# Regrouped out-projection rows, a new order of the last projection chunks and GpSimd remainders in a four-layer attention and Fourier kernel

## The chip, the cores and the metric

The kernel runs on one core of a Trainium2 chip. The metric is device time in microseconds (us) of one execution; lower is better. [...] TensorE (PE in the profile) multiplies, VectorE (DVE), ScalarE (ACT) and GpSimd (POOL) do elementwise work, and SyncE (SP) issues all the DMAs of this kernel from one queue, in order. Each engine takes its own instructions in the order in which the program lists them.

## The reference

Four layers on one sequence of 2048 rows of 640 numbers, all in float32: attention, Fourier, attention, Fourier, each with a residual.

```python
def _A_ref(x, wqkv, wo):
    B, S, D = x.shape
    H = 32; Dh = D // H; W = 256
    ...
    scores = jnp.einsum("bhqd,bhkd->bhqk", q, k) * (Dh ** -0.5)
    ...
    mask = (idx[:, None] - idx[None, :] >= 0) & (idx[:, None] - idx[None, :] < W)
    scores = jnp.where(mask[None, None], scores, -1e9)
    p = _softmax(scores, axis=-1)
    o = jnp.einsum("bhqk,bhkd->bhqd", p, v)
    return (lambda x, *d: x.transpose(*d))(o, 0, 2, 1, 3).reshape(B, S, D) @ wo
...
x = x + _A_ref(_layernorm(x, axis=-1), A_wqkv, A_wo)
x = x + _B_ref(_layernorm(x, axis=-1), B_dft_seq_re, B_dft_seq_im, B_dft_hid_re, B_dft_hid_im)
```

`_B_ref` is a Fourier mix: a product with two 640x640 matrices, then with two 2048x2048 matrices, and the real part. The change lies in the attention layers alone.

## The kernel before, in words

**Products.** Each float32 operand is kept as a high part, rounded to the matmul's fp32r, and a remainder (`lo = x - hi`); a product is three matmuls, hi*hi, hi*lo and lo*hi. To make such a pair, one engine casts and another subtracts: `split` (L220) does both at once, `cut_job` (L212) queues the cast on ScalarE and then, by `sub_job` (L198), the subtract on VectorE ("dve") or on GpSimd ("pool", there in two halves of the columns).

**The attention layer.** `before_heads` (L364) normalizes, transposes, makes the values v and chunks 0 and 1 of the q and k projection. `heads` (L597) holds the rest. The 32 heads go in 8 quads of four. A quad has 16 query blocks of 128 rows, and the loop over `step` (L770) handles one block a step: at step t the scores of block t+10 with rows as output (`s_head`, L617, matmul L622, running row maximum on VectorE at L627), the transposed scores of block t (`t_pair`, matmul L650), their exponential on ScalarE (`t_exp`, L660), the band mask on GpSimd (`t_mask`, L666 and L670), and for block t-1 the product with v (`pv`, matmul L685, copied out at L692). 128 steps plus 10 ahead make the stage. Scores and values share six PSUM banks, and the order in which they are taken is written down by a small planner (`borrow`, L136) with assumed holding times. After four blocks `finish` (L696) stores the quad's unnormalized output (`od`) and the reciprocal of its sums (`rd`) and notes (quad, block of 512 columns) in `stored`.

**Fill.** Between these matmuls `fill` (L745) puts others that the heads do not wait for. `more` (L731) takes them from three generators in turn. `project` (L559) makes the remaining chunks 2 to 9 of q and k, each for four column blocks of 512 (sb 0 to 3), two blocks at a time (`pieces`, L523): 30 pairs of matmuls (L253), about four a step. `partials` (L946) multiplies the first three of five 128-row chunks of the attention output by their rows of the output weights, for 16 tiles of 128 sequence rows, and adds x (L970). `late` (L1024) adds the other two chunks, then normalizes for the Fourier layer. What remains of `late` after the last step runs in `after_heads` (L1103) among the first Fourier matmuls (L1360). `due` (L717) says at which step which part of the projection has to be done, since `pack` (L573) reloads q and k of a quad, two chunks wide, eight steps before their use.

**A finished piece** (`copied`, L537): ScalarE copies it out of PSUM (L540) to one of five raw tiles (`raw`, L158), GpSimd casts it (L543), VectorE subtracts (L207), SyncE stores it (L520) and `packable` is noted.

**Queued work.** `tick` (L172) runs once per half step. It runs what `post` (L166) has put off by so many half steps, and then takes at most one job from each of three lanes, ScalarE, VectorE and GpSimd. Since engines take instructions in order, a job's place in this order is its place in the engine's queue.

**Chunks of the attention output.** Its 640 rows are sorted into five chunks of 128 (`CHUNKS`, L45) as rectangles of heads by coordinates. `load_o` (L835) loads one chunk for one block (L855) with the reciprocals broadcast to the same rows (L861), scales it in two halves on GpSimd (L885) seven half steps later, and cuts it. It waits until all quads of the chunk are in `stored`: chunks 0 and 1 need quads 0 to 3, chunk 2 quads 4 and 5, chunk 3 quads 6 and 7, chunk 4 all eight. Two sets of buffers serve blocks 0 and 1, and then again blocks 2 and 3. `prepare` (L909) loads the weights for the partial products when chunk 9 begins, cuts them and asks for block 0 when chunk 9's second half begins, and loads the first four tiles of x when the projection ends (`load_y`, L941).

## Time and profile before

| | us |
|---|---|
| median of 3 runs | 2223.3 (2220.41 to 2227.0) |
| the profiled execution | 2220.75 |
| its span, first to last instruction | 2219.0 |
| mean granted TensorE clock | 0.991 |
| first attention layer, head steps 0 to 127 | 159.22 to 535.59 |
| second attention layer, head steps 0 to 127 | 1260.74 to 1636.29 |

A row of a windows view has the stretch in us from the span's start and its length, then the busy time of TensorE's matmuls, of its weight loads, of VectorE, ScalarE and GpSimd, each with its number of instructions in brackets, and last the granted clock of TensorE (1.00 is full), the mean busy share of the 16 DMA engines and their GB/s. A row of a group has line, engine and operation, out<-in with the shapes, the count, then busy us and mean ns of one, and the idle time before it with what ended it. In the view of a single line the three numbers are the shortest, median and longest duration in ns. In a waits view the three numbers are total us, times and the longest one. A timeline row has start, duration, engine, line.

### The profile page before, as it was taken

How to read it: one execution, taken by the hardware profiler on the slowest of the kernel's cores; microseconds unless marked ns; L12 is line 12 of the kernel's file. 1: busy time of each engine (PE TensorE's matmuls, PEld its weight loads, DVE VectorE, ACT ScalarE, POOL GpSimd, SP SyncE). 2: the span in 40 equal slices, each digit the busy share in tenths (PEclk: the TensorE clock that was granted, in tenths of full speed). 3: DMA queues.
4: the chain of work that ended last, by engine and by line, in shares of the span. 5: the costliest groups of instructions: out<-in, count | busy, mean ns of one | idle time of the engine just before them, and what ended most of it. 6: DMA issues, size and time to landing. Idle time of an engine off the chain costs nothing.

```text
span 2219.0 us, 49084 instructions
## 1 busy us (share of the span) xinstructions
PE 2131.4 (96%) x17908; PEld 1786.0 (80%) x17908; DVE 1669.5 (75%) x4031; ACT 1126.6 (51%) x2101; POOL 910.6 (41%) x1456
## 2 busy tenths in 40 slices
PE   7999999998989999999999999998989999999999
PEld 7987777677868888889999777776777688888899
DVE  7368888785897968776651788887858978687776
ACT  3127776656554545552431377676655545455332
POOL 3016565666613223232330266566665132341334
PEclk9999999899999999999999999999999999999999
DMA  5545565775435354665646456657855354546653
GB/s 196 176 160 190 182 190 192 225 208 175 142 124 176 128 185 133 215 202 193 205 147 191 151 189 183 199 184 225 211 160 157 115 182 137 174 143 216 223 169 120
DMA packets 220177, 392.11 MB, mean 177 GB/s; under 512 B 39200, under 2 KB 85792, under 8 KB 219936
## 3 DMA queue, kind: packets, MB, share of 16 engines
q1 hardware_dynamic: 219936, 388.98, 55.6%
q8 instruction: 141, 2.31, 0.5%
q14 instruction: 100, 0.82, 0.1%
HBM read 273.94 MB, written 113.77 MB: 175 GB/s over the span
## 4 chain that ended last, share of the span: by engine, by line
PE 70%; DVE 13%; issue 6%; DMA 4%; ACT 3%; POOL 3%; SPq 0%; ACTq 0%; DVEq 0%; POOLq 0%
PE banks L1360 28%; PE banks L235 13%; PE banks L253 9%; PE banks L685 5%; PE banks L650 5%; DVE banks L627 5%; PE banks L1648 4%; PE banks L622 4%; DMA qp<-qk_d 1%; DVE c L207 1%; POOL big L228 1%; DVE mc L627 1%; DMA qk_d<-c 1%; DVE qp L228 1%; PE banks L337 1%
## 5 line engine op out<-in xcount | busy, mean ns | idle before, releaser
L627 DVE CUSTOM_DVE_ANT_0 banks<-banks,mask 128x384 f32<-128x384 f32 (+2 forms) x1024 | 526.8, 556 | 98.5 <-PE banks L622 80.5
L660 ACT ACTIVATE pt<-banks 128x768 f32<-128x768 f32 (+2 forms) x512 | 394.3, 772 | 179.0 <-PE banks L650 74.0
L666 POOL TENSOR_SCALAR_AFFINE_SELECT pt<-pt 128x256 f32<-128x256 f32 x512 | 215.8, 422 | 282.0 <-ACT pt L660 243.2
L253 PE MATMUL banks<-big,wc 64*128 64x512 f32 x1920 | 271.2, 394 | 0.4 <-DVE pt L438 0.4
L650 PE MATMUL banks<-qp,kp 61*128 61x384 f32 (+2 forms) x1024 | 211.8, 383 | 32.5 <-DVE mc L627 28.5
L685 PE MATMUL banks<-pt,vq 128*32 128x128 f32 x5760 | 213.4, 280 | 1.5 <-ACT pt L660 1.5
L622 PE MATMUL banks<-kp,qp 60*128 60x384 f32 (+2 forms) x1024 | 204.9, 352 | 6.6 <-DVE mc L627 4.1
L670 POOL TENSOR_SCALAR_AFFINE_SELECT pt<-pt 128x256 f32<-128x256 f32 x448 | 207.2, 462 | 0.0
L253 PEld LDWEIGHTS banks<-big,wc 64*128 64x128 f32 x1920 | 186.5, 185 | 22.9 <-ACT x L540 1.7
L650 PEld LDWEIGHTS banks<-qp,kp 61*128 61x128 f32 x1024 | 108.6, 186 | 100.4 <-DVE mc L627 76.5
L685 PEld LDWEIGHTS banks<-pt,vq 128*32 128x32 f32 x5760 | 143.4, 110 | 49.5 <-issue 36.4
L222 ACT ACTIVATE c<-pt 128x512 fp32r<-128x512 f32 x150 | 93.6, 626 | 160.3 <-POOL pt L1280 52.9
L222 ACT ACTIVATE qp<-pt 128x512 fp32r<-128x512 f32 (+1 forms) x195 | 119.9, 624 | 105.3 <-DVE pt L1294 54.0
L228 DVE TENSOR_TENSOR c<-pt,c 128x512 fp32r<-128x512 f32 x150 | 123.0, 822 | 52.0 <-ACT c L222 49.9
L228 DVE TENSOR_TENSOR qp<-pt,qp 128x512 fp32r<-128x512 f32 (+1 forms) x191 | 151.2, 799 | 11.7 <-ACT qp L222 9.0
L1360 PE MATMUL banks<-qp,big 128*128 128x512 f32 x630 | 152.4, 394 | 2.9 <-POOL qp L228 1.7
L1293 POOL TENSOR_TENSOR pt<-pt,pt 128x512 f32<-128x512 f32 x34 | 50.7, 1490 | 237.1 <-DMA pt<-c 145.9
L622 PEld LDWEIGHTS banks<-kp,qp 60*128 60x128 f32 x1024 | 119.9, 188 | 32.1 <-DVE mc L627 19.5
L627 DVE DVE_READ_ACCUMULATOR2_ANT mc<- 128x1 f32 x1024 | 144.3, 141 | 0.0
L1360 PEld LDWEIGHTS banks<-qp,big 128*128 128x128 f32 x630 | 119.0, 190 | 28.8 <-POOL qp L228 2.3
L1360 PE MATMUL banks<-qp,xc 128*128 128x512 f32 x480 | 117.2, 390 | 0.7 <-DVE xc L228 0.7
L543 POOL CAST c<-x 128x512 fp32r<-128x512 f32 x64 | 40.3, 633 | 181.3 <-ACT x L540 180.3
(246 smaller groups left out, 4475.0 us busy)
## 6 DMA issues: line engine op xcount, KB each, us to landing
pt<-c SPq DMA_DIRECT2D x188, 512.0 KB
qk_d<-c SPq DMA_DIRECT2D x80, 512.0 KB
kp<-qk_d SPq DMA_DIRECT2D x384, 80.0 KB
qp<-qk_d SPq DMA_DIRECT2D x384, 80.0 KB
kp<-u_d SPq DMA_DIRECT2D x32, 640.0 KB
o_d<-ou SPq DMA_DIRECT2D x64, 256.0 KB
x_d<-x SPq DMA_DIRECT2D x48, 320.0 KB
v_d<-pt SPq DMA_DIRECT2D x16, 768.0 KB
```

The lines of the kernel that those rows point to most:

```text
L222: nc.scalar.activation(hi, src, AF.Copy, scale=-1.0 if neg else 1.0)
L228: (eng or nc.vector).tensor_tensor(out=lo, in0=src, in1=hi.bitcast(F32), op=OP.subtract)
L235: self.nc.tensor.matmul(p, x, y, start=n == 0, stop=n == last)
L253: self.nc.tensor.matmul(ps[a], x[r], y[r], start=half + i == 0, stop=half == 1 and i == n - 1, skip_group_check=True)
L622: nc.tensor.matmul(p, qp[quad % 2][b:b + 60, z, qb * P:(qb + 1) * P], kp[quad % 2][b:b + 60, z, k0 * P:(qb + 1) * P], start=True, stop=True)
L627: nc.vector.tensor_tensor_reduce(out=p, in0=p, in1=self.mask[:, 384 - n * P:], scale=1.0, scalar=NEG, op0=OP.add, op1=OP.max, accum_out=mc ...
L650: nc.tensor.matmul(self.banks[:, banks[e], :n * P], kp[quad % 2][b:b + 61, z, kb * P:(kb + 1) * P], qp[quad % 2][b:b + 61, z, kb * P:(kb + ...
L660: nc.scalar.activation(pt[quad, kb][:, 2 * z:2 * z + 2, :n * P], self.banks[:, b0:b1 + 1, :n * P], AF.Exp, scale=SCALE)
L666: nc.gpsimd.affine_select(out=t[:, :, 0:P], in_=t[:, :, 0:P], pattern=[[0, 2], [1, P]], compare_op=OP.is_ge, fill=0.0, base=0, channel_mul ...
L670: nc.gpsimd.affine_select(out=t[:, :, 256:384], in_=t[:, :, 256:384], pattern=[[0, 2], [-1, P]], compare_op=OP.is_gt, fill=0.0, base=0, ch ...
L685: nc.tensor.matmul(self.banks[32 * h:32 * h + 32, bank, :P], vq[:, 96 * (kb % 4) + 21 * h:96 * (kb % 4) + 21 * h + 32], t[:, h, (qb - kb) ...
L1360: nc.tensor.matmul(self.banks[:, bk, :], p, b[q], start=start and m == 0, stop=stop and last and m == 2, skip_group_check=True)
```

## The change

Six things change, all in the attention layers.

1. The rows are sorted anew. A chunk is now one or two rectangles, and the first three chunks need quads 0 to 4 only; chunk 3 needs quads 4 to 6, chunk 4 quads 5 to 7. The rows of the output weights follow.
2. The last two projection chunks go by halves: blocks 0 and 1 of chunks 8 and 9, then blocks 2 and 3 of both (`LAST`). The due times follow this order.
3. A finished piece is cast on ScalarE and its remainder made on GpSimd in two halves, each a job of the lane; so are the weights' remainders (there undivided), those of all early chunks and of the late weights. The late chunks are scaled and cut on VectorE instead.
4. A raw tile is held until its reader is done (`hold`), and `hold` runs half steps of queued work until the tile is free.
5. The requests for early weights and chunks stand in a queue of their own, one leaving per half step when two raw tiles are free. They start when block 2 of chunk 8 begins, blocks 0 and 1 together; block 2 is asked for in partial tile 1, block 3 in tile 5.
6. Before step -2 a lane gives two jobs per half step.

```diff
-CHUNKS = ((0, 16, 0, 8), (0, 16, 8, 16), (16, 24, 0, 16), (24, 32, 0, 16), (0, 32, 16, 20))
+CHUNKS = (((0, 16, 0, 8),), ((0, 16, 8, 16),), ((0, 16, 16, 20), (16, 20, 0, 16)),
+          ((16, 20, 16, 20), (20, 28, 0, 14)), ((20, 28, 14, 20), (28, 32, 0, 20)))
+
+LAST = [(c, sbs) for sbs in ((0, 1), (2, 3)) for c in (NCH - 2, NCH - 1)]
...
+    def room(self, n=1):
+        return not any(self.raw_n + i - XS in self.raw_held for i in range(n))
+
+    def hold(self):
+
+        while not self.room():
+            self.tick()
+        n = self.raw_n
+        self.raw_held.add(n)
+        return self.raw(), lambda: self.raw_held.discard(n)
...
+        if self.asks and self.room(2):
+            self.asks.popleft()()
         for lane in self.lanes.values():
-            if lane and lane[0][0] <= self.slot:
-                lane.popleft()[2]()
+            for _ in range(2 if self.lead else 1):
+                if lane and lane[0][0] <= self.slot:
+                    lane.popleft()[2]()
...
-        n = 2 if lane == "pool" else 1
+        n = 2 if lane == "pool" and len(src.shape) == 2 else 1
...
-            for ks in (slice(0, 3), slice(3, KC)):
-                self.cut_job("dve", ("w", c), w[:, 0, ks], w[:, 1, ks], raw[:, ks])
+            for ks, done in ((slice(0, 3), None), (slice(3, KC), free)):
+                self.cut_job("pool", ("w", c), w[:, 0, ks], w[:, 1, ks], raw[:, ks], done)
...
-            def cast():
-                self.nc.gpsimd.tensor_copy(st[:, 0, :], r)
-                self.sub_job("dve", ("qk", c, sb), st[:, 1, :], r, st[:, 0, :],
-                             lambda: self.post(2, store))
+            def lead():
+                if self.c_live == 3:
+                    self.post(1, lambda: self.job("act", key, lead))
+                    return
+                self.c_live += 1
+                st = self.work.tile([P, 2, 512], F32R, name="c", tag="c", bufs=3)
+                self.nc.scalar.activation(st[:, 0, :], r, AF.Copy)
+                self.sub_job("pool", key, st[:, 1, :], r, st[:, 0, :], lambda: (free(), self.post(1, lambda: store(st))))
...
-        for c in range(2, NCH):
+        for c in range(2, NCH - 2):
...
+        for c, sbs in LAST:
+            if (c, sbs) == LAST[0]:
+                self.cut_chunk(NCH - 1)
+            if (c, sbs) == LAST[2]:
+                self.prepare(2)
+            yield from self.pieces(c, sbs, "m")
         self.prepare(4)
...
+        for h0, h1, d0, d1 in rects:
+            nh, nd = h1 - h0, d1 - d0
+            rs = slice(r0, r0 + nh * nd)
+            r0 += nh * nd
+            src = self.od[h0:h1, 1 + d0:1 + d1, cols]
+            nc.sync.dma_start(raw[rs], src if nh >= nd else src.rearrange("h d s -> d h s"))
+            if not shared:
+                src = self.rd[sb, h0:h1, :]
+                nc.sync.dma_start(rr[rs], src.unsqueeze(1).broadcast_to([nh, nd, 512]) if nh >= nd else
+                                  src.unsqueeze(0).broadcast_to([nd, nh, 512]))
...
+        lane, n, wait = ("pool", 2, 7) if k < EARLY else ("dve", 1, 4)
+        eng = nc.gpsimd if k < EARLY else nc.vector
 
         def parts():
+            if k < EARLY and self.part_t < 4 * (sb - 1):
+                self.post(1, parts)
+                return
             hi, lo = o[k]
-            self.cut_job("pool" if k == 0 else "dve", key, hi, lo, raw, lambda: self.post(0 if k < EARLY else 3, done))
+            self.cut_job(lane, key, hi, lo, raw, lambda: self.post(0 if k < EARLY else 1, done))
...
+            self.ask(0, self.load_early)
+            self.ask(1)
...
+    def load_early(self, k):
+        raw, free = self.hold()
+        self.nc.sync.dma_start(raw, self.a["wo"][:, k, :])
+        self.early_cut += 1
+
+        def cut():
+            self.early_cut -= 1
+            self.cut_job("dve", "ew", *self.early_w[k], raw, free)
+        self.post(4, cut)
+
+    def ask(self, sb, also=None):
+        o = self.early_o[sb % 2]
+        o["left"] = o.get("left", 0) + EARLY
+        for k in range(EARLY):
+            def one(k=k):
+                o["left"] -= 1
+                self.load_o(o, sb, k)
+            if also:
+                self.asks.append(lambda k=k: also(k))
+            self.asks.append(one)
...
-            if sb + 1 < NSB and i == 0:
-                for k in range(2):
-                    self.load_o(sets[(sb + 1) % 2], sb + 1, k)
+            if t in (1, 5):
+                self.ask(t // 4 + 2)
...
+                self.post(4, lambda k=k, raw=raw: self.cut_job("pool", "lw", *self.late_w[k - EARLY], raw))
```

More of the change, by code (lines that the diff above doesn't have):

```diff
@@ L33 @@
 AHEAD_X = 4
+XS = 5
 AFTER = 4
@@ L99, in __init__ @@
         self.posted = {}
+        self.raw_n, self.raw_held, self.asks = 0, set(), deque()
         self.lanes = {n: deque() for n in ("act", "dve", "pool")}
@@ L537, in copied, with store @@
         def copied(p, sb):
-            st = self.work.tile([P, 2, 512], F32R, name="c", tag="c", bufs=3)
-            r = self.raw()[:, :512]
+            r, free = self.hold()
+            r = r[:, :512]
+            key = "qk", c, sb
             self.nc.scalar.activation(r, p, AF.Copy)
-            def cast():
-                self.nc.gpsimd.tensor_copy(st[:, 0, :], r)
-                self.sub_job("dve", ("qk", c, sb), st[:, 1, :], r, st[:, 0, :],
-                             lambda: self.post(2, store))
-            def store():
+            def lead():
[6 more added lines that the diff above has]
+                self.sub_job("pool", key, st[:, 1, :], r, st[:, 0, :], lambda: (free(), self.post(1, lambda: store(st))))
+            def store(st):
                 self.store_qk(c, sb, st)
+                self.c_live -= 1
                 self.packable.add((c, sb))
-            self.job("pool", ("qk", c, sb), cast)
+            self.job("act", key, lead)
         for r in self.lockstep(sets):
@@ L837, in load_o @@
         nc = self.nc
-        h0, h1, d0, d1 = CHUNKS[k]
+        rects = CHUNKS[k]
+        quads = sorted({h // 4 for h0, h1, _, _ in rects for h in range(h0, h1)})
         o["left"] = o.get("left", 0) + 1
-        if not self.after and not all((q, sb) in self.stored for q in range(h0 // 4, h1 // 4)):
+        if not self.after and not all((q, sb) in self.stored for q in quads):
             def again():
@@ L845, in load_o @@
             return
-        for q in range(h0 // 4, h1 // 4):
+        for q in quads:
             while (q, sb) not in self.stored:
@@ L912, in prepare @@
         ks = range(EARLY)
-        if n == 0:
-            self.early_w = []
-            raws = cuts(self.work.tile([P, 2 * D], F32, name="we", tag="wc"), D) + [None]
-            raws[2] = self.raw()
-            for k in ks:
-                nc.sync.dma_start(raws[k], a["wo"][:, k, :])
-            self.early_raw = raws
-        elif n == 2:
+        if n == 2:
             self.take_big(0)
-            self.early_w += pairs(cuts(self.big[0], D))[:EARLY]
-            for k in (2, 0, 1):
-                self.cut_job("dve", "ew", *self.early_w[k], self.early_raw[k])
+            self.early_w = pairs(cuts(self.big[0], D))[:EARLY]
             self.take_big(1)
@@ L939, in prepare @@
             self.load_y(range(AHEAD_X))
+    def load_early(self, k):
+        raw, free = self.hold()
+        self.nc.sync.dma_start(raw, self.a["wo"][:, k, :])
[14 more added lines that the diff above has]
+            self.asks.append(one)
     def load_y(self, ts):
```

87 lines of the change are left out of this document (40 added, 47 removed).

## The prediction

> **What bounds the kernel now.** I read the page first: its head and the first row of its first part.
>
> ```profile
> span 2219.0 us, 49084 instructions
> PE 2131.4 (96%) x17908; PEld 1786.0 (80%) x17908; DVE 1669.5 (75%) x4031; ACT 1126.6 (51%) x2101; POOL 910.6 (41%) x1456
> ```
>
> TensorE counts as busy for 96%, but that is a mean over stages, so I cut the span into stretches of head steps. A step is the time from one exponential (L660) of a key block to that of the next block. The next rows are windows of layer 0: head steps 64 to 79, 80 to 91, 92 to 98, 99 to 111 and 118 to 127, and steps 92 to 98 of layer 1.
>
> ```profile
> core 0: us, PE busy (x) PEld busy (x) DVE busy (x) ACT busy (x) POOL busy (x), PEclk, DMA share, GB/s
> ...
> 338.08:382.79 44.71, 43.15 (x616) 32.59 (x614) 38.50 (x140) 31.70 (x58) 26.92 (x64) 1.00 0.61 194
> 382.79:417.03 34.24, 32.81 (x456) 24.36 (x452) 29.79 (x107) 27.36 (x48) 25.09 (x57) 1.00 0.67 204
> 417.03:443.27 26.24, 22.91 (x242) 15.73 (x242) 18.52 (x63) 12.28 (x25) 12.71 (x28) 0.67 0.81 237
> 443.27:486.98 43.71, 40.66 (x657) 34.16 (x655) 36.39 (x123) 26.54 (x49) 30.16 (x63) 1.00 0.76 199
> ...
> 507.41:535.59 28.18, 26.35 (x442) 21.62 (x442) 10.03 (x20) 19.59 (x37) 23.05 (x46) 1.00 0.37 113
> ...
> 1518.39:1543.76 25.37, 20.29 (x242) 14.00 (x242) 18.41 (x63) 12.22 (x25) 12.68 (x28) 0.87 0.76 223
> ```
>
> The reader is to see a hole. Steps 99 to 111 hold 657/13 = 50.5 matmuls each, steps 92 to 98 of both layers only 242/7 = 34.6: the projection has ended, the first partial out-products are not ready, and the steps run without fill. They are no shorter for it: 26.24/7 = 3.75 us and 25.37/7 = 3.62 us against 43.71/13 = 3.36 us with fill. The granted clock is 0.67 and 0.87 there, and in layer 1 the waits of this stretch show a stall:
>
> ```profile
> DVE rc L705 <- DMA sm<-ou: 3.1, 1, 3.1
> ```
>
> The reciprocal held VectorE, in order, for 3.1 us until a small DMA landed behind the first four loads of y.
>
> Inside the even part, single steps of quad 3 show the second limit (windows of one step; the fifth is a step without anything extra):
>
> ```profile
> 301.32:303.95 2.63, 2.63 (x41) 1.80 (x37) 2.51 (x9) 2.63 (x7) 2.07 (x6) 1.00 0.26 91
> 303.95:307.33 3.38, 2.93 (x44) 2.21 (x43) 3.38 (x12) 2.64 (x6) 3.21 (x6) 1.00 0.52 162
> 307.33:310.41 3.08, 2.79 (x44) 2.03 (x42) 2.99 (x12) 1.90 (x3) 1.54 (x4) 1.00 1.01 364
> ...
> 315.89:318.48 2.59, 2.59 (x42) 2.03 (x42) 2.39 (x9) 1.90 (x4) 1.26 (x4) 1.00 0.64 198
> ...
> 326.65:330.04 3.39, 2.94 (x44) 2.21 (x43) 3.39 (x11) 1.94 (x5) 3.22 (x6) 1.00 0.76 228
> ```
>
> In the long steps VectorE is busy from end to end (3.38 of 3.38, 2.99 of 3.08, 3.39 of 3.39): there the remainders of finished projection pieces and of the next weights are subtracted. Over 2.59 us they cost 0.79 + 0.49 + 0.80 = 2.08 us a quad.
>
> Last, behind the heads, two windows in each layer:
>
> ```profile
> 535.59:549.23 13.64, 9.50 (x87) 8.12 (x79) 8.61 (x22) 4.70 (x10) 4.96 (x8) 1.00 0.89 276
> 549.23:557.11 7.88, 7.25 (x25) 6.43 (x26) 6.13 (x21) 5.61 (x11) 4.23 (x6) 0.57 0.69 235
> ...
> 1636.29:1649.94 13.65, 9.50 (x88) 8.12 (x80) 8.63 (x22) 4.70 (x10) 4.97 (x8) 0.98 0.86 269
> 1649.94:1656.50 6.56, 6.56 (x22) 6.11 (x23) 4.93 (x16) 5.29 (x11) 2.92 (x5) 0.52 0.74 246
> ```
>
> TensorE is idle for 13.64 - 9.50 = 4.1 us while the late set of block 1 is scaled and cut, and then runs 7.88 us at a clock of 0.57, which loses 3.4 us. Layer 1 is alike: 4.1 and 3.1 us.
>
> **The change, part by part.** Its durations, from the groups by line and from the views of single lines:
>
> ```profile
> L207 DVE TENSOR_TENSOR c<-x,c x20: 814/834/874, 192.2 to 394.8; 128x512 fp32r<-128x512 f32 x20
> ...
> L207 POOL TENSOR_TENSOR big<-x,big 128x256 fp32r<-128x256 f32 x6 | 4.4, 737 | 0.0
> ...
> L215 ACT ACTIVATE big<-x 128x512 fp32r<-128x512 f32 x9 | 5.6, 623 | 1.7 <-POOL x L885 1.7
> ...
> L692 ACT ACTIVATE ou<-banks 128x128 f32<-128x128 f32 x31 | 8.6, 277 | 6.1 <-PE banks L685 5.0
> ...
> L540 ACT ACTIVATE x<-banks x64: 592/599/616, 134.6 to 1517.8; 128x512 f32<-128x512 f32 x64
> ...
> L543 POOL CAST c<-x x64: 605/611/985, 135.3 to 1519.1; 128x512 fp32r<-128x512 f32 x64
> ```
>
> *Term 1, remainders of the projection.* A piece loses one VectorE subtract (0.83 us) and one GpSimd cast (0.61), and gains one ScalarE cast (0.62) and two GpSimd half subtracts (2 x 0.74). The weights' remainders move as well. If nothing took VectorE's place, 2.08 us a quad would go: the projection lasts 92 steps, 5.75 quads, in two layers, so 23.9 us. That is the upper end. Against it stands ScalarE. The cast is queued for the same half step as the copy out of PSUM, between two exponentials (0.81 us each). One half step is then 0.81 + 0.60 + 0.62 = 2.03 us, the other with the copy of `ou` 0.81 + 0.60 + 0.28 + 0.62 = 2.31: 4.34 us in a step that now takes 2.63 with ScalarE already full. These two timeline rows show that TensorE waits for an exponential already when one copy stands before it:
>
> ```profile
> 257.37 0.59 ACT L540 ACTIVATE x<-banks 128x512 f32<-128x512 f32 x1
> 257.52 0.18 PEld L622 LDWEIGHTS banks<-kp,qp 60*128 60x128 f32 x1 [0.17 <-ACT pt L660]
> ```
>
> With no catching up, a set (two pieces, two sets a quad) costs 4.34 - 2.63 = 1.71 us, and a quad loses 2 x 1.71 - 2.08 = 1.34: 15.4 us in all, the lower end. With full catching up, ScalarE's work in the three steps decides: 2.63 + 2.64 + 1.90 + 1.25 = 8.42 us against 2.63 + 3.38 + 3.08 = 9.09 now, a gain of 0.67. I take 0, near the middle, because the exponential's bank is wanted almost at once but the two steps behind it have 0.7 and 1.2 us of ScalarE time free.
>
> *Term 2, GpSimd's queue.* These rows of the page's fifth part give the masks:
>
> ```profile
> L666 POOL TENSOR_SCALAR_AFFINE_SELECT pt<-pt 128x256 f32<-128x256 f32 x512 | 215.8, 422 | 282.0 <-ACT pt L660 243.2
> ...
> L670 POOL TENSOR_SCALAR_AFFINE_SELECT pt<-pt 128x256 f32<-128x256 f32 x448 | 207.2, 462 | 0.0
> ```
>
> That is (215.8 + 207.2)/256 = 1.65 us a step. One job leaves the lane per half step, so while it holds jobs a step asks 1.65 + 2 x 0.74 = 3.13 us of GpSimd, 0.5 more than a basic step lasts. Masks stand in the same queue and the value products wait for them. The slack is the time from a step's last mask to its first value product:
>
> ```profile
> 253.66 0.41 POOL L670 TENSOR_SCALAR_AFFINE_SELECT pt<-pt 128x256 f32<-128x256 f32 x1
> ...
> 255.26 0.64 PE L685 MATMUL banks<-pt,vq 128*32 128x128 f32 x16
> ```
>
> That is 255.26 - 254.07 = 1.2 us. The four half jobs of one set (lag 1.0) fit. From about step 77, where the early sets are now asked for, to step 92 they do not: 12 half jobs for block 0, about 3 for block 1 and some 9 of the projection make 24, 12 steps, 6.2 us of lag a layer, of which slack and gaps between jobs hide about half. I take -3 a layer, -6; ends 0 and -12.4. The store of a finished piece now waits for GpSimd's second half, and behind it in SyncE's queue stand the reloads of q and k and the small loads of sums; they have steps of slack, so I cost that at nothing, and a reciprocal that stalls again is rival B. Likewise `hold`, which runs queued work early when all five raw tiles are taken: requests wait until two are free. The late weights' remainders, four half jobs near step 115, hide under steps that TensorE bounds; uncovered they are 4 x 0.74 = 3 us a layer, inside the lower end.
>
> One row speaks on GpSimd's side: a mask beside a VectorE subtract took twice its time.
>
> ```profile
> 258.90 0.87 DVE L207 TENSOR_TENSOR c<-x,c 128x512 fp32r<-128x512 f32 x1
> ...
> 259.18 0.86 POOL L670 TENSOR_SCALAR_AFFINE_SELECT pt<-pt 128x256 f32<-128x256 f32 x1
> ```
>
> [...]
>
> *Term 3, the hole.* The early chunks now need quads 0 to 4 instead of 0 to 5, so their data is stored 16 steps sooner, and big0 and big1 come free 8 steps sooner since blocks 0 and 1 are projected first. Block 0 (six of the nine first requests, through five raw tiles, a chunk about 12 half steps) should be cut by step 89, before the projection ends at 92. Seven filled steps at 3.36 us are 23.5 a layer, against 26.24 and 25.37: a gain of 4.6. Ends 0 (the stall on the reciprocal stays, since the y loads still come at the projection's end) and 9 (no step over 3.03).
>
> *Term 4, the tail.* Six steps of fill come sooner, so the partial products end near step 122 instead of 127. The late set then finds room in the heads: its chunks wait 4 half steps instead of 7 and are scaled and cut on VectorE, idle there (10.03 of 28.18 us). I expect three of its sixteen tiles inside the heads; one is the 12 matmuls of this row:
>
> ```profile
> 571.69 1.92 PE L235 MATMUL banks<-qp,kp 128*128 128x320 f32 x12
> ```
>
> That is 5.8 us of TensorE work moved, and the wait for block 1 starts sooner. At most the idle and half-clock loss goes, 7.5 + 7.2 = 14.7; at least nothing, if block 3's chain (last quad, reciprocal, reload) is what the end waits for. I take 4 a layer, 8, near the middle.
>
> *Term 5, long steps of the partial stage.* Where VectorE cuts two of three chunks, steps stand out (against 3.40 just before):
>
> ```profile
> 456.48:459.88 3.40, 3.09 (x56) 2.69 (x54) 2.62 (x11) 2.41 (x5) 2.96 (x6) 1.00 0.47 124
> 459.88:463.91 4.03, 2.63 (x46) 2.17 (x46) 3.83 (x11) 1.89 (x5) 3.52 (x7) 1.00 0.80 201
> ...
> 466.94:470.56 3.62, 3.53 (x55) 2.88 (x56) 3.01 (x9) 2.05 (x4) 1.89 (x5) 1.00 1.07 284
> ...
> 486.98:491.02 4.04, 3.09 (x54) 2.57 (x52) 3.74 (x11) 1.90 (x3) 2.49 (x5) 1.00 0.99 297
> ```
>
> They are 0.63 + 0.22 + 0.64 us over; 3.0 in two layers. GpSimd's 3.13 us fits into 3.36, so I take +3; the other end is -3, the same steps made as long by GpSimd.
>
> *Term 6, pieces of chunks.* Chunks 2, 3 and 4 load by two rectangles each: six DMA issues more a block.
>
> ```profile
> 568.98 1.49 SPq L855 DMA_DIRECT2D pt<-o_d  x1
> 570.52 0.60 SPq L861 DMA_DIRECT2D vq<-r_d  x1
> ```
>
> At 0.60 us each they hide behind other work of SyncE's queue, save four of the last block: 2.4 us a layer at most. I take -1, ends 0 and -5.
>
> Sum: 0 - 6 + 4.6 + 8 + 3 - 1 = 8.6 us of gain. The profiled execution took 2220.75 us, 1.75 more than its span and 2.55 less than the median 2223.3; 2220.75 - 8.6 gives **2212 us**.
>
> **Rivals.** *A, slower:* the queues of ScalarE and GpSimd take VectorE's place. Terms 1 and 2 cost their lower ends, the tail gives half: -15.4 - 12.4 + 4.6 + 4 + 3 - 1 = -17.2, 2238 us. For it speaks that TensorE waits after one copy already; against it that ScalarE was full in step 301.32:303.95 and that step is not longer. It decides from where a set's step grows by more than the 1.04 us that the set saves.
>
> *B, no change:* the hole is filled, but the reciprocal's stall returns and the late chain still ends last: 0 - 6 + 2 + 0 + 3 - 1 = -2, 2223 us. For it: DMA share 0.81 and 0.76 in the hole, and the loads move rather than vanish.
>
> *C, much faster:* ScalarE catches up. Sets give 0.67 and, without weights (steps 11 to 13 of a quad, alike), about 0.8: 1.5 x 5.75 x 2 = 17; with -3 + 4.6 + 10 + 3 - 1 that is 31, 2190 us.
>
> *D, the clock stays low:* in layer 0 the hole's 26.24 us at 0.67 lose 8.7 us of clock though TensorE is busy for 22.91 of them. If that drop comes whatever fills the steps, the filled steps pay it: 2212 + 8.7 = 2221 us. [...] Layer 1 speaks for fill: its unfilled steps kept the full clock until the stall.
>
> **How the numbers follow.** Chances: forecast 0.37 (its own range 2203 to 2220), A 0.27, B 0.13, C 0.17, D 0.06. About 0.3%, 6.7 us on the median, is what a measurement of this kernel can tell from no change: faster is under 2216.6, slower over 2230. Faster: 0.34 of the forecast, 0.17 of C and 0.02 of the others, 0.53. Slower: A and 0.02 of B, 0.29. Same: the rest, 0.18. The range reaches from a little past C, 2188, to a little past A, 2240; the ends of all terms together (2170 to 2257) are wider, and I leave them out as unlikely together.
>
> **What would show it.** Steps 92 to 98 hold about 50 matmuls each at a clock of 1.00 (term 3). No step of quads 0 to 4 has VectorE full; the step with the copies is longer than 2.63, ScalarE full in it (term 1). GpSimd is full from step 78 to 92 and value products wait for L670 (term 2). The window of 20 us behind the heads is shorter and has three late tiles fewer (term 4). I am wrong if the steps after a set stay near 3.4, if the hole is still there, or if new waits of TensorE for SyncE's transfers appear.

## The result, and the profile after

The changed kernel takes 2235.6 us (median of 4 runs, 2235.4 to 2236.0) against 2223.4 for the kernel before in the same session (4 runs, 2220.4 to 2227.0): the ratio is 1.0055, with a 95% interval of 1.0037 to 1.0072. It is slower, by more than the 0.3% that can be told from no change; 2212 had been forecast. The profiled execution took 2236.0 us.

These rows stand for the whole span: the page's head, and the four exponential groups of the two kernels, one for each layer's heads (first and last start behind the durations; before is L660, after L694).

```profile
span 2234.3 us, 49112 instructions
```

```profile
L660 ACT ACTIVATE pt<-banks x256: 355/812/854, 159.2 to 535.2; 128x768 f32<-128x768 f32 x112, 128x512 f32<-128x512 f32 x8, 128x256 f32<-128x256 f32 x8
...
L660 ACT ACTIVATE pt<-banks x256: 357/812/854, 1260.7 to 1635.9; 128x768 f32<-128x768 f32 x112, 128x512 f32<-128x512 f32 x8, 128x256 f32<-128x256 f32 x8
```

```profile
L694 ACT ACTIVATE pt<-banks x256: 356/811/834, 160.5 to 548.9; 128x768 f32<-128x768 f32 x112, 128x512 f32<-128x512 f32 x8, 128x256 f32<-128x256 f32 x8
...
L694 ACT ACTIVATE pt<-banks x256: 356/811/835, 1269.2 to 1656.3; 128x768 f32<-128x768 f32 x112, 128x512 f32<-128x512 f32 x8, 128x256 f32<-128x256 f32 x8
```

The heads grew from 376.0 to 388.4 us in layer 0 and from 375.2 to 387.1 in layer 1. From the last exponential to the next layer's first, or to the span's end, the time fell: 725.5 to 720.3, and 583.1 to 578.0. So +12.4 +11.9 -5.2 -5.1, and 1.3 us later into the first heads: 15.3, the difference of the spans. What was meant for the tail came; the heads lost more than twice as much.

Where in the heads? The windows of the prediction once more, of the changed kernel: layer 0, steps 64 to 79, 80 to 91, 92 to 98, 99 to 111; then steps 92 to 98 of layer 1.

```profile
core 0: us, PE busy (x) PEld busy (x) DVE busy (x) ACT busy (x) POOL busy (x), PEclk, DMA share, GB/s
340.68:388.18 47.50, 45.46 (x625) 33.81 (x621) 37.25 (x139) 34.46 (x62) 28.92 (x68) 1.00 0.65 193
388.18:428.51 40.33, 34.98 (x449) 25.34 (x451) 27.04 (x101) 28.66 (x53) 32.74 (x70) 0.96 0.65 193
428.51:456.49 27.98, 22.26 (x327) 18.70 (x325) 18.49 (x65) 13.01 (x26) 17.05 (x36) 0.94 0.82 257
456.49:499.34 42.85, 40.76 (x657) 34.17 (x655) 34.44 (x120) 26.81 (x49) 34.65 (x72) 1.00 0.74 208
...
1535.62:1564.74 29.12, 23.04 (x327) 19.19 (x325) 18.49 (x65) 13.02 (x26) 17.05 (x36) 0.88 0.80 249
```

The hole is filled: 327 matmuls where there were 242. Yet these steps are longer, 27.98 and 29.12 us against 26.24 and 25.37, and the twelve steps ahead of them, where the prediction had priced GpSimd's queue alone (term 2, 3 us a layer), went from 34.24 to 40.33. Single steps stand out in both layers: 89 and 90 (5.8 and 4.6 us, 6.3 and 4.1 in layer 1), 93 and 94 (7.8 and 4.5, 8.2 and 5.2). The waits of the engines between 405 and 450 us, and SyncE's timeline (SPq, its issues of transfers), say on what:

```profile
PE banks L684 <- DVE mc L661: 5.0, 2, 4.6
DVE big L1030 <- DMA big<-x: 4.5, 1, 4.5
...
PE banks L684 <- DMA qp<-mt: 2.8, 1, 2.8
```

```profile
410.95 0.37 SPq L542 DMA_DIRECT2D qk_d<-c  x1
411.85 0.53 SPq L907 DMA_DIRECT2D x<-o_d  x1
414.96 1.50 SPq L619 DMA_DIRECT2D kp<-qk_d  x3
416.56 0.39 SPq L542 DMA_DIRECT2D qk_d<-c  x1
417.04 1.46 SPq L674 DMA_DIRECT2D qp<-mt  x2
```

Two things are late. SyncE stands from 412.4 to 415.0 at the reload of a projection chunk (L619) whose store it issued at 410.95, and the row maxima (L674), which TensorE needs at step 90, stand behind it. At step 93 the first partial add (L1030) waits 4.5 us at the head of VectorE's queue for y, which can only be fetched when the projection has let go of its buffer; the score reductions queue behind it, and TensorE behind them (4.6 us).

### The profile page after: what moved, and what is told of

It reads as the page before. It is cut to its first block, busy times and chain, and to the rows that moved or that the text cites. A ratio compares the mean times of both kernels' runs of the same rounds, so it can differ in the third digit from the quotient of the medians.

```text
span 2234.3 us, 49112 instructions
## 1 busy us (share of the span) xinstructions
PE 2137.6 (96%) x17944; PEld 1787.5 (80%) x17944; DVE 1605.3 (72%) x3925; ACT 1159.8 (52%) x2161; POOL 968.1 (43%) x1572
## 5 line engine op out<-in xcount | busy, mean ns | idle before, releaser
L694 ACT ACTIVATE pt<-banks 128x768 f32<-128x768 f32 (+2 forms) x512 | 393.6, 770 | 177.2 <-PE banks L684 81.1
L700 POOL TENSOR_SCALAR_AFFINE_SELECT pt<-pt 128x256 f32<-128x256 f32 x512 | 210.8, 412 | 251.1 <-ACT pt L694 223.0
L684 PE MATMUL banks<-qp,kp 61*128 61x384 f32 (+2 forms) x1024 | 209.9, 381 | 34.4 <-DVE mc L661 23.5
L656 PE MATMUL banks<-kp,qp 60*128 60x384 f32 (+2 forms) x1024 | 210.6, 351 | 11.4 <-ACT pt L694 10.5
L704 POOL TENSOR_SCALAR_AFFINE_SELECT pt<-pt 128x256 f32<-128x256 f32 x448 | 182.9, 408 | 0.0
L656 PEld LDWEIGHTS banks<-kp,qp 60*128 60x128 f32 x1024 | 124.8, 187 | 44.0 <-ACT pt L694 27.1
L227 POOL TENSOR_TENSOR c<-x,c 128x256 fp32r<-128x256 f32 x128 | 94.1, 741 | 44.1 <-ACT c L571 41.9
```

The lines of the kernel that those rows point to most:

```text
L227: eng.tensor_tensor(out=lo[..., c], in0=src[..., c], in1=hi[..., c].bitcast(F32), op=OP.subtract)
L656: nc.tensor.matmul(p, qp[quad % 2][b:b + 60, z, qb * P:(qb + 1) * P], kp[quad % 2][b:b + 60, z, k0 * P:(qb + 1) * P], start=True, stop=True)
L684: nc.tensor.matmul(self.banks[:, banks[e], :n * P], kp[quad % 2][b:b + 61, z, kb * P:(kb + 1) * P], qp[quad % 2][b:b + 61, z, kb * P:(kb + ...
L694: nc.scalar.activation(pt[quad, kb][:, 2 * z:2 * z + 2, :n * P], self.banks[:, b0:b1 + 1, :n * P], AF.Exp, scale=SCALE)
L700: nc.gpsimd.affine_select(out=t[:, :, 0:P], in_=t[:, :, 0:P], pattern=[[0, 2], [1, P]], compare_op=OP.is_ge, fill=0.0, base=0, channel_mul ...
L704: nc.gpsimd.affine_select(out=t[:, :, 256:384], in_=t[:, :, 256:384], pattern=[[0, 2], [-1, P]], compare_op=OP.is_gt, fill=0.0, base=0, ch ...
```

## The experiments

Theory 1: two single waits, new with the order and the earlier start. Its rival: the prediction's A, the queues of ScalarE and GpSimd. Both were widened as results came in. Each run's ratio is to the kernel before in its own session, with its interval. The steps quoted for a run are those of its profiled execution, which can lie several us off the median.

**Order undone.** `LAST` lists chunk 8's two halves and then chunk 9's; the cut and `prepare(2)` move with it.

```
-LAST = [(c, sbs) for sbs in ((0, 1), (2, 3)) for c in (NCH - 2, NCH - 1)]
+LAST = [(c, sbs) for c in (NCH - 2, NCH - 1) for sbs in ((0, 1), (2, 3))]
```

> The changed kernel with one part undone: the last two projection chunks run one after the other again (chunk 8 on blocks 0-1, 2-3, then chunk 9), not by halves; everything else as changed. Theory (two new waits at the end of the projection: the reload of chunk 8's third block right after its store, which holds SyncE for 2.5 us ahead of the row maxima, and the first partial add, which waits 4.5 us in VectorE's queue for y): the chunk is stored 8 steps earlier again, so step 89-90 fall from 5.8 + 4.6 to about 2.8 us each; the sets come 8 steps later, so the partial products start behind a gap and the y wait goes too. Quads 4 and 5 lose 8 to 11 us a layer: 2215 to 2224 us, with quad 7 and the tail a few us longer if the earlier sets were what shortened them. Rival (the queues of ScalarE and GpSimd, filled by the remainders): the order has nothing to do with it, 2232 to 2238 us.

Measured 2244.4 us, 1.0089 (1.0074 to 1.0104): a miss of both, slower still. Step 89 fell to 2.9 us in both layers, but step 90 stayed at 4.6 and 3.8, and step 97 took 5.3 and 6.3. Its two groups of exponentials:

```profile
L694 ACT ACTIVATE pt<-banks x256: 356/810/830, 158.7 to 542.5; 128x768 f32<-128x768 f32 x112, 128x512 f32<-128x512 f32 x8, 128x256 f32<-128x256 f32 x8
...
L694 ACT ACTIVATE pt<-banks x256: 357/811/830, 1275.0 to 1657.6; 128x768 f32<-128x768 f32 x112, 128x512 f32<-128x512 f32 x8, 128x256 f32<-128x256 f32 x8
```

The heads do get shorter (383.8 and 382.6 us, from 388.4 and 387.1), but behind them 1275.0 - 542.5 = 732.5 us go by instead of 720.3: the order by halves costs some 4.5 us a layer in the heads and is what pays behind them.

**Reload put off.**

```
-defer(i // 3, f)
+defer(i // 3 + (2 if q == NQ - 2 and j > 1 else 0), f)
```

> The changed kernel; only the reloads of quad 6, blocks 2 and 3, are queued two steps later, so that the chunk 8 they read has been stored when SyncE comes to them. Theory: SyncE's wait of 2.5 us for the stored chunk and TensorE's 2.8 us for the row maxima go, with them 4 to 5 us a layer at steps 89-90: 2225 to 2228 us, steps 93-94 (7.8 + 4.5 us) unchanged. Rival (queues of ScalarE and GpSimd): within 2 us of 2235.6. A third way: the transfers of step 89 were late for a full DMA queue and not for the wait; then the wait moves on by two steps and the time stays.

Measured 2229.3 us, 1.0018 (1.0002 to 1.0034). Steps 89 and 90 fell to 3.0 + 3.2 and 3.1 + 3.1, as theory 1 has it. The wait for y stayed:

```profile
DVE big L1030 <- DMA big<-x: 4.5, 1, 4.5
```

**Start of the partial products put off** by 6 half steps from the moment that the y loads are queued (the hold, in what follows).

```
+            self.post(6, lambda: setattr(self, "y_in", True))
-        return t == NB or t % 4 or not (self...
+        return t == NB or t % 4 or self.y_in and not (self...
```

> The changed kernel; only the partial products may not begin before 6 half steps have gone by since the y loads were queued (three steps with no fill, as in the kernel before). Theory: the first partial add no longer stands in VectorE's queue for y; steps 93-94 fall from 12.3 to about 6 us, less the time that three steps' products (about 3 us) cost elsewhere if the later steps have no room: 4 to 6 us a layer, 2224 to 2228 us; step 89-90 unchanged. Rival (queues of ScalarE and GpSimd): no change or up to 3 us slower, 2235 to 2239, since work is put off. Rival (the hole itself is dear, as the prediction's term 3 had it): slower by 1 to 2 us a layer.

Measured 2229.3 us, 1.0023 (1.0007 to 1.0038). Steps 93 and 94 went from 12.3 to 7.6 us, but in layer 0 steps 101 and 102 now took 7.8 + 5.7, where TensorE waits for the next row maxima (440 to 475 us):

```profile
PE banks L684 <- DMA qp<-mt: 4.4, 1, 4.4
```

**Remainders as before.** GpSimd rounds, VectorE subtracts (pieces and chunk weights).

> The changed kernel with the remainders as before: rounding of a set on GpSimd, remainders of sets and chunk weights on VectorE in one piece, store two half steps after; order, regrouping and the output products' edits as changed. Theory (the two waits): steps 89-90 and 93-94 keep their excess; VectorE takes back the 3 sets' work that ScalarE and GpSimd had, worth nothing to 3 us a layer either way: 2230 to 2241 us. Rival (the prediction's A: the remainders' queues on ScalarE and GpSimd are the cost): 2218 to 2226 us.

Measured 2236.9 us, 1.0048 (1.0032 to 1.0064), against 1.0055 (1.0037 to 1.0072) with the change whole. The remainders of pieces and chunk weights are not the cause. Against the expectation, steps 89 and 90 did not keep their excess: they took 3.0 + 3.2 us in both layers, and step 85 took 7.2 and 7.1 instead. The early chunks are still cut on GpSimd in this run, which stays busy for 31.12 of 39.96 us in steps 80 to 91. Against GpSimd's part of rival A speak the waits of the changed kernel: in steps 78 to 111 TensorE waited for a mask once a layer, for 0.3 us.

**Cuts of the early weights later** (`self.post(4, cut)` to 8).

> The changed kernel; only the cuts of the early weights are queued 8 half steps after their loads, not 4. Theory: ScalarE no longer stands 1.9 us at the head of its queue for wo; steps 78-83 (3.6, 4.5, 3.9, 3.7 in layer 0) fall by 1 to 3 us a layer in all, the rest stays: 2230 to 2234 us. Rival (their length is the cuts' own work on VectorE and ScalarE): no change, 2235 to 2237; slower by more than 2 us if the later weights hold the first partial product back.

Measured 2235.9 us, 1.0047 (1.0030 to 1.0063). Steps 78 and 79 fell from 3.6 + 4.5 to 3.0 + 2.5 in layer 0, and step 93 rose from 7.8 to 12.3. A wait removed early came back later, and theory 1 as a list of separate waits began to fall.

**Row maxima from ScalarE's queue, and three mends in one.** In quads 5 and 6 `nc.scalar` issues them; the second kernel adds the hold for y and the later weights.

> The changed kernel; only the row maxima of quads 5 and 6 (qp<-mt, 16 small transfers a layer) are issued from ScalarE's queue instead of SyncE's. Theory 1 (SyncE's in-order queue, held behind the reload of a chunk just stored, makes the row maxima late): steps 89-90 fall from 5.8 + 4.6 (layer 0) and 6.3 + 4.1 (layer 1) to about 3.0 + 3.2, as where the reload was put off; the other steps stay, ScalarE pays 16 issues of at most 0.6 us: 3 to 4 us a layer less, 2227 to 2230 us. Rival (it was the reload itself, or its transfers, that was late, not the order in SyncE's queue): 2235 to 2238 us. If ScalarE's queue is itself the bound here (the prediction's A), its issues make steps 80-110 longer: 2236 to 2245.

> The changed kernel with three mends together: row maxima of quads 5 and 6 from ScalarE's queue, the partial products held back 6 half steps for y, and the early weights' cuts queued 8 half steps after their loads, not 4. Theory (late transfers in SyncE's queue at three places): steps 89-90, 93-94 and 78-83 lose their excess, and the second wait for row maxima at step 101 that the hold alone showed (7.8 + 5.7 us) goes as well: 10 to 12 us a layer of which the hold gives 2 or 3 back behind the heads: 2214 to 2219 us. Rival (the queues of ScalarE and GpSimd): 2228 or more, no more than the single mends gave.

Measured 2269.7 us, 1.0196 (1.0180 to 1.0213), and 2262.9, 1.0163 (1.0148 to 1.0178): misses. Between 380 and 470 us of the first, SyncE and ScalarE wait thus:

```profile
SPq L542 <- DMA qp<-mt: 6.9, 1, 6.9
```

```profile
ACT big L235 <- DMA x<-wo: 6.4, 2, 6.2
```

ScalarE pays ten issues of 0.52 us there and now stands 6.2 us for wo at the head of its queue, with the exponentials behind it. SyncE stood 6.9 us, at a store (L542), for one of ScalarE's transfers, with which it shares no data: it waited for that transfer's semaphore, of which more below. As a test of theory 1 they are void: they put a new wait where the old one had been. So is a third kernel, these three mends with the old remainders: 2257.4 us, 1.0143 (1.0128 to 1.0158), 5.5 us under the three mends where at most 3 had been expected.

By now a count of SyncE's issues over steps 78 to 112 showed the same 1.6 to 1.7 a us in both kernels. That is theory 2: the stage is as long as SyncE's queue. The next runs left work out, or took issues off that queue.

**A third of the reloads of quads 6 and 7 left out** (the third 20 rows, so that these heads read old rows), in the changed kernel, in the kernel before, and in the changed kernel for quads 2 to 7. The eight reloads left of twelve are queued two a step instead of three.

```
+                    if quad >= NQ - 2 and part == 2:
+                        continue
```

> The changed kernel with work left out: of the reloads of quads 6 and 7, four of the twelve transfers a block (the third 20 rows of qp and kp) aren't issued, so the scores of these quads use old rows there. Theory 2 (SyncE's rate of issue is the bound of the stage): in the kernel before it issued 93 and 86 transfers in steps 78-96 in 54.5 and 51.0 us, in the changed one 112 and 111 in 66.8 and 66.2 us, which is 1.68 to 1.71 a us in all four. Some 16 fewer in steps 78-96 and 12 to 16 fewer in 96-112 at that rate are 16 to 19 us a layer: 2197 to 2210 us, until another engine binds. Theory 1 (two waits of their own at steps 89-90 and 93-94): the reload behind the stored chunk is still there, 0 to 4 us a layer: 2227 to 2236 us.

> The kernel before with the same work left out (four of the twelve reloads a block of quads 6 and 7). Theory 2 (SyncE's rate is the bound of steps 78-112 in the kernel before too): 9 + 8 us a layer less, 2188 to 2200 us. Theory 1 (SyncE had room before, and only the change's waits are SyncE's): 0 to 3 us a layer, 2217 to 2224 us.

> As where four of twelve reloads of quads 6 and 7 are left out of the changed kernel, but for quads 2 to 7. It asks where SyncE's rate begins to bind. In steps 64-78 the two kernels already issue 66 to 69 transfers in 39.1 to 39.5 us, 1.7 a us. If that is SyncE's limit, quads 1 to 4, of 44.6 to 45 us, fall by up to 9 us each: 2130 to 2170 us. If these quads are bound by something else (TensorE, VectorE and the steps' own order) and 1.7 a us is only what they ask for, they stay at 44.6 to 45 us, and the time is that of the run with quads 6 and 7 alone, within 5 us.

Measured 2220.2 us, 0.9975 (0.9964 to 0.9986); 2213.3, 0.9958 (0.9942 to 0.9974); 2220.6, 0.9983 (0.9966 to 0.9999). Steps 78 to 111 as one window, layer 0 and where shown layer 1 (us, TensorE clock, DMA share, GB/s): the kernel before, the changed one, the kernel before with less, the changed one with less.

```profile
377.24:486.98 109.74, 0.92 0.76 218
...
1478.64:1587.62 108.98, 0.97 0.77 215
```

```profile
380.10:499.34 119.24, 0.97 0.74 220
...
1488.98:1607.75 118.77, 0.96 0.74 218
```

```profile
380.80:484.58 103.78, 1.00 0.69 203
```

```profile
380.13:492.00 111.87, 0.98 0.69 208
```

Both kernels gain, 6.0 us and 7.4 us in layer 0. So the kernel before was already held by transfers in these steps, and the change, whose 9.5 and 9.8 us a layer lie here, asked more of them. Where they gain is seen in steps 92 to 98, both layers, of the kernel before with less and of the changed one with less:

```profile
420.82:441.13 20.31, 17.25 (x242) 11.75 (x242) 18.51 (x63) 12.12 (x25) 12.63 (x28) 1.00 0.82 244
1517.18:1537.47 20.29, 17.20 (x242) 11.74 (x242) 18.51 (x63) 12.10 (x25) 12.63 (x28) 1.00 0.82 248
```

```profile
425.60:449.48 23.88, 21.05 (x327) 17.34 (x325) 18.46 (x65) 13.01 (x26) 17.05 (x36) 1.00 0.85 265
1529.24:1552.54 23.30, 20.90 (x327) 17.36 (x325) 18.46 (x65) 13.02 (x27) 17.05 (x36) 1.00 0.83 258
```

The kernel before gains in the hole alone: its unfilled steps, with the same 242 matmuls, go from 26.24 and 25.37 us to 20.3 and from a clock of 0.67 and 0.87 to 1.00. They had been long for late transfers, and for the low clock that went with these, not for want of fill. The filled steps of the changed kernel come to 23.88 and 23.30 us. The two kernels stay 8.1 and 8.5 us a layer apart: 3.6 and 3.0 of it is the fill, and 5.5 and 6.5 lie in steps 78 to 91, where step 79 still took 5.4 and 5.9 us.

From quad 2 on the same cut gains nothing more: steps 48 to 77 take as long with less traffic (the changed kernel, and the third kernel here).

```profile
295.91:380.10 84.19, 1.00 0.61 183
```

```profile
297.76:382.36 84.60, 1.00 0.50 155
```

**Three transfers put off in SyncE's queue**, nothing left out: reloads and y as above, and the second set's loads 16 half steps later.

> The changed kernel with nothing left out and three transfers put off in SyncE's queue: reloads of quad 6, blocks 2 and 3, two steps later; the second early set's loads 16 half steps after the first's; the partial products 6 half steps after the y loads are queued. Theory 1 (single waits): both excesses go, 8 to 10 us a layer of heads, 2 to 3 given back behind them: 2218 to 2224 us. Theory 2 (rate): the same transfers are to be issued by step 112, so a wait moves to steps 97-105: 2224 to 2231 us, no more than the single mends. Rival (queues of ScalarE and GpSimd): 2233 or more.

Measured 2228.5 us, 1.0006 (0.9995 to 1.0017): no difference from the kernel before that can be told, and no better than either single mend beyond their intervals. Steps 101 and 102 (7.2 + 5.5 us in layer 0, 5.8 + 4.9 in layer 1) took the wait over, as theory 2 had it. They are read from a long execution: 2236.0 us, the longest of the ten.

**Fewer issues for the same bytes:** 16 y loads as 5, in the changed kernel with the hold, and in the kernel before.

> The changed kernel with the hold of 6 half steps for y, and the 16 y loads of a layer issued as 5 (2, 2, 4, 4 and 4 tiles each): the same bytes, 10 issues fewer in steps 78-112, nothing left out. Theory 2 (SyncE's issues, at most some 1.7 a us, are the bound of steps 78-112): 10 / 1.7 = 6 us a layer less than the hold alone (2229.3): 2215 to 2222 us. Theory 1 (single waits) or bytes as the bound: within 3 us of the hold alone, 2226 to 2232; slower if the larger transfers land later than the hold covers.

> The kernel before, with only its 16 y loads of a layer issued as 5. Theory 2: 8 of the 184 issues in its steps 78-112 are saved, 4 to 5 us a layer: 2213 to 2217 us. Theory 1 (SyncE is late only where the change made it so): 2222 to 2225 us.

Measured 2238.6 us, 1.0064 (1.0042 to 1.0086), and 2233.8, 1.0047 (1.0031 to 1.0064): slower, against theory 2. In the second, SyncE's waits from 431 to 492 us begin with

```profile
SPq L585 <- DMA big<-x: 7.8, 2, 4.6
```

a reload that waits for a load of y, with which it shares no data. The traces have why: in this program SyncE's transfers signal by eight semaphores in turn, and no issue started before the transfer eight places ahead of it had landed (all 1866 such issues of the kernel before, all 1914 of the changed one). A load of y keeps its place for longer than a reload: in steps 78 to 111 of the kernel before, layer 0, a reload of 80 KB (kp) landed 3.2 us after its issue in the median of 48, a load of y of 320 KB 5.1 us in that of 13. The longest of SyncE's waits for a load of y was 1.8 us there, against 4.6 us with four tiles a load. With the 5 loads, all three transfers put off as above took 2234.7 us, 1.0049 (1.0030 to 1.0067), where theory 2 had expected 2214 to 2222: a miss too, with 9.7 + 5.0 us in steps 101 and 102.

**y issued by GpSimd, tile by tile,** which takes 16 issues a layer out of SyncE's queue (changed kernel with the hold; kernel before).

> The changed kernel with the hold of 6 half steps for y, and the 16 y loads of a layer, one tile each as they were, issued by GpSimd's queue instead of SyncE's; nothing left out. In steps 78-112 SyncE's 200 transfers took 91 us to issue and 25 us of waits at its queue's head, of 119 us. Theory 3 (SyncE's queue is full there: issuing plus waits make up the stage): 15 issues less, at 0.42 to 0.5 us each, and 2 to 4 us of waits for the landing of y go: 8 to 10 us a layer below the hold alone (2229.3), less what a y load costs GpSimd in front of its masks: 2212 to 2222 us. If GpSimd pays over 1 us for each issue in a stage where it is 60 to 80% busy: 2225 to 2240. Rival (bytes or single waits are the bound): within 3 us of the hold alone.

> The kernel before, with only its 16 y loads of a layer issued by GpSimd's queue. Theory 3: its SyncE was as full in steps 78-112 (82 us of issuing and 27 of waits in 110 us), so 13 issues less and 3 us of waits for the y landings give 5 to 9 us a layer: 2205 to 2214 us, less GpSimd's own cost. Rival (only the change made SyncE late): 2222 to 2225 us. If GpSimd's issue is dear: 2225 to 2240.

Measured 2233.5 us, 1.0036 (1.0024 to 1.0049), and 2225.3, 1.0009 (0.9998 to 1.0021). No gain, although an issue costs GpSimd only 0.57 us. Steps 78 to 111 of the kernel before with y on GpSimd, layers 0 and 1, take about as long in sum as without (109.74 and 108.98):

```profile
379.55:488.03 108.48, 0.98 0.77 222
...
1481.73:1593.27 111.54, 0.97 0.77 216
```

Nor did GpSimd's issues eat the gain: in these steps TensorE waited for a mask once, in layer 0, for 0.2 us. So SyncE's issuing is not the bound: fewer transfers help (0.9958 in the kernel before), the same transfers issued elsewhere do not (1.0009). What is left, though no run shows it by itself, is their landing.

**Old grouping of the rows** in the changed kernel (one rectangle a chunk, six quads early).

> The changed kernel with one part undone: the out-projection's rows grouped as before (the early chunks need six quads; a set takes 5 issues, not 7; the late ones 4, not 8). Order by halves, remainders, queueing as changed. Theory 2: the sets can't be fetched before quad 5 is stored, so they are issued about 8 steps later and with 8 issues fewer up to step 112: steps 78-96 fall to about 55-58 us a layer (from 66), the first partial add comes at step 97 or 98; heads 376 to 382 us (388), and behind the heads 4 to 7 us come back: 2222 to 2232 us. Theory 1: the reload behind the stored chunk (order) stays with its 4 to 5 us a layer, the y wait goes: 2226 to 2230 us; told apart by steps 89-90 (10.4 us or about 6).

Measured 2238.6 us, 1.0067 (1.0042 to 1.0091). Steps 89 and 90 came down to 2.9 + 3.0 in layer 0 and 3.9 + 3.1 in layer 1 with the order still by halves, so the order by itself does not make the reload behind its store that dear; steps 97 and 98 took 9.8 + 5.2 instead in layer 0 (4.2 + 4.9 in layer 1). No late tile is left inside the heads, and the gain behind them is gone.

## Why the prediction was wrong, point by point

**Term 1 (remainders: 0): right.** Quads 1 to 3 went from 44.6 - 44.9 us to 44.7 - 45.0, some 1 us in all against 0. Quad 0 grew by 0.9 and 1.0, but it is as long (45.5 and 45.6) with the old remainders, so that is not theirs. As worked out, ScalarE takes VectorE's place; steps 51 to 53 of the changed kernel:

```profile
303.76:307.58 3.82, 3.46 (x45) 2.28 (x43) 2.81 (x11) 3.79 (x8) 2.07 (x6) 1.00 0.37 110
307.58:310.23 2.65, 2.63 (x39) 1.78 (x39) 1.86 (x9) 2.41 (x6) 2.25 (x5) 1.00 0.69 197
310.23:312.79 2.56, 2.56 (x44) 2.00 (x42) 2.28 (x9) 1.90 (x4) 2.56 (x7) 1.00 0.85 288
```

ScalarE is full in the first (3.79 of 3.82), and the next two make up for it: 9.03 us against 9.09. The run with the old remainders agrees.

**Term 2 (GpSimd's queue: -6): the right engine load, no visible cost.** GpSimd went to 32.74 of 40.33 us in steps 80 to 91 (25.09 of 34.24 before), but no wait of TensorE there ends on a mask, and giving the remainders of pieces and weights back gained nothing. On its other side the masks became faster, 462 to 408 ns (456 with the old remainders):

```profile
L700 POOL TENSOR_SCALAR_AFFINE_SELECT pt<-pt 128x256 f32<-128x256 f32 x512 | 210.8, 412 | 251.1 <-ACT pt L694 223.0
...
L704 POOL TENSOR_SCALAR_AFFINE_SELECT pt<-pt 128x256 f32<-128x256 f32 x448 | 182.9, 408 | 0.0
```

In the kernel before, 57 of the 448 masks of L670 took over 0.6 us, all of them among the 73 that ran beside a VectorE subtract (L207); in the changed kernel one of the 448 of L704 took so long. Why a mask takes longer there, no run shows.

**Term 3 (the hole: +4.6): the step that failed.** The sets were there and the steps were filled, as said. But the term put the hole's 26.24 and 25.37 us down to missing fill, and left the loads out. The price of "seven filled steps at 3.36 us", 23.5, was right: with fewer reloads they took 23.88 and 23.30. What it was set against was wrong: without late transfers the unfilled steps take 20.3, so that filling them costs 3.6 and 3.0 us in this place and gains nothing there. With all reloads the filled steps were 1.7 and 3.8 us longer than unfilled, and steps 80 to 91, ahead of them, lost 6.1 more in layer 0. What covered the y loads was the hole itself: it gave them six steps before the first add. With the hole gone the add waits, in front of the scores. The lower end, 0, named one small wait (the reciprocal) and not that a transfer that can only start at the projection's end becomes the first thing that is late.

**Term 4 (the tail: +8): right, a little small.** The last partial add came at step 123 instead of 128. Six late adds, two for a tile, lie inside the heads in each layer: the three tiles foreseen. 5.2 and 5.1 us came, against 4 a layer. It rests on the order by halves: undone, it loses this and more.

**Term 5 (+3):** steps 99 to 111 went from 43.71 to 42.85 us in layer 0 and from 43.86 to 43.01 in layer 1: the right sign, 1.7 of 3.

**Term 6 (more transfers: -1): mis-sized, for the same reason.** It counted added issues behind the heads. What counts is what falls into steps 78 to 111. Rate times time of the windows above gives 218 x 109.74 = 23.9 MB before and 220 x 119.24 = 26.2 after: 2.3 MB more in layer 0 and about as much in layer 1: early weights, y, set data and, in layer 0, a store that had stood in other steps. At some 219 GB/s, the rate of both kernels there, 2.3 MB take 10.5 us, about the 9.5 and 9.8 that the stage grew. That is an agreement and no proof: the stage also took in the fill of the hole.

**Rivals.** The time is near A's 2238 us, but that is luck: the old remainders gained nothing (1.0048), and TensorE hardly waited for GpSimd. B had the right words, "the loads move rather than vanish", with the wrong wait and price. The text's last sign of being wrong, new waits of TensorE for SyncE's transfers, is what appeared. D did not decide: the clock in steps 92 to 98 rose, 0.67 to 0.94 and 0.87 to 0.88, and the time did not follow. Nor is missing fill what lowers the clock: with fewer reloads the unfilled steps ran at 1.00.

**What stays open.** Shown is that most of the loss, 9.5 of 12.4 us and 9.8 of 11.9, lies in steps 78 to 111, that taking single late transfers out of the way gains 6 to 8 us and all three together not clearly more (7 to 11), and that fewer reloads make both kernels faster. That the bytes themselves are the bound was only argued: single windows reach 257 GB/s, and with the order undone the stage, steps 78 to 111 of layer 0, was this:

```profile
378.79:494.57 115.78, 0.87 0.73 204
```

That is 204 x 115.78 = 23.6 MB, no more than the 23.9 of the kernel before, in 6 us more. The changed kernel with fewer reloads is another case: 208 x 111.87 = 23.3 MB, in 2 us more than the kernel before. Order and landing time matter beside the sum of bytes, and no run separates them. Loading the early weights before step 78, as the kernel before did, beside the order by halves was not tried. No version that leaves nothing out beat the kernel before.

## What to carry to other kernels

Before filling a hole, list which transfers land in it: their cover goes with the hole, and each can become a wait in the in-order queue of whoever uses it first. Ask, too, whether the hole is long for want of fill or for those transfers: leave some of them out and time it unfilled. When work is moved earlier, its loads move too; sum the bytes and issues of the stage that they move into, and if leaving some out there makes the old kernel faster, that stage already waits for transfers. One late transfer mended in such a stage can hand its wait to the next, so mends must be timed together.

## What the runs showed of the hardware

- With this program's eight semaphores SyncE had at most eight transfers under way: an issue waited for the landing of the one eight places ahead, whatever it carried (1866 of 1866 in the kernel before, 1914 of 1914 in the changed one). With loads of y four tiles large a reload stood 4.6 us for one, and the kernel before lost some 11 us (2233.8 against 2222.2) with eleven issues fewer a layer.
- The same 16 loads of y cost GpSimd 0.57 us an issue; taken off SyncE they changed the time of the kernel before by some 0.2% at most (1.0009, 0.9998 to 1.0021).
- Sixteen small transfers a layer issued by ScalarE instead of SyncE cost some 31 us in all (1.0196 against 1.0055), of which the 32 issues, 0.50 to 0.64 us each in ten of them, make some 20 at most; waits of 6.2 us on ScalarE and 6.9 us on SyncE came with them.
